# T2 to T4 of the inner values made in place by GpSimd in a pair's second half, and the last pair's splits put in front

## The chip, the core and the metric

The kernel runs on one core of one Trainium2 chip. A core has a matrix engine (TensorE, in the rows PE, its weight loads PEld), a vector engine (VectorE, DVE), a scalar engine (ScalarE, ACT), GpSimd (POOL), and a sync engine (SP) that here only issues DMAs. Each engine takes its own instructions in order; semaphores tie the engines together. Operands lie in SBUF, results of matmuls in PSUM. The metric is the device time of one execution in microseconds; less is better. Three runs of the kernel before gave 1194.9, 1196.52 and 1198.41 us, median 1196.52.

## The reference

Attention in chunks of 64 tokens, then two feed-forward layers over 4608 tokens, all in float32:

```python
scores = scale * q_c @ k_c^T ; attn = softmax(scores) ; x = attn @ v_c      # x: 4608 x 512
h = x @ w_in                                                                # 512 -> 2048
g = h * clip(h + 3, 0, 6) / 6
x = g @ w_out                                                               # 2048 -> 512
h = x @ w_in2 ; solu = h * softmax(h) ; ln = layernorm(solu) * g_ln         # 512 -> 1024
out = ln @ w_out2                                                           # 1024 -> 512
```

## The kernel before

**Precision.** Every float32 operand of a matmul is split into a high part (ScalarE copies it to the faster fp32r type) and a low part (source minus high part, on VectorE or GpSimd). A product is then three matmuls: high by high, high by low, low by high.

**Stages.** The 4608 tokens are 9 blocks of 512. Blocks 0 to 2 go through the first layer plainly (lines 1619 to 1710). Beside their work the kernel forms sums of weight quarters (`sums_of`, `split_sums`) and stores them in HBM (`sti`, `sto`). Blocks 3 to 8 are three pairs, and a pair's first layer is done by Strassen's scheme in Winograd's form: seven products in place of eight. The first two pairs go through `pair_7`, the third through `pair`; then comes the second layer.

**`pair_7`, first half** (line 1356, j from 0 to 7). Seven products per j (`mul7`, line 1164) give four hidden tiles of 128 x 512, which pass through the gate and become the inner values B11, B12, B21 and B22. The second matrix w_out also takes a seven-product form, so the inner values need Winograd's sums as well: T1 = B12 - B11, T2 = B22 - T1, T3 = T2 - B11, T4 = B21 - T2. `later_sums` (line 1335) makes the four on GpSimd as soon as a j is through; T1 stays in SBUF, T2 to T4 go to HBM (`later_t`) by SP's queue.

**`pair_7`, second half** (line 1423). Seven products i, each over eight j. Two j are one wide piece of 128 x 1024, so there are 28 pieces, numbered d = 0 to 27, four to a product. `prepare(d)` splits a piece: ScalarE copies the high part (line 1285), VectorE subtracts for the low part (line 1286); for the pieces 20, 23 and 26 in two halves (1282, 1283). It is issued three pieces ahead of use. `mul_o` (line 1301) then spends 12 matmuls on a piece; the third matmul is the first that reads the low part. `bring` (line 1291) loads T2, T3 and T4 back from HBM into the slots `wo` that the pieces used before have left (`HOMES`). Ten closures in `todo` (made by `prep`, line 1193) are popped at the places in `steps`: they split and subtract the next pair's inputs, on ScalarE (line 1181) and VectorE (1182, 1201). Attention for later blocks is strewn in (`stage`, `att_slot`): transposes on VectorE (490, 494), exponentials on ScalarE (448), scaling on GpSimd (465).

**`pair`, the third pair.** Its w_out products are plain (`moe_o`, line 574), with weights that `load_o` brings from `sto` into the slots `wo`. In the idle places of VectorE and ScalarE it prepares the second layer's weights: `Second.window(words, small)` works on chunks that come by DMA into `xr` (lines 155, 258, 261, 295, 302, 319). What is left of `todo` when it begins is two closures, the splits of B22 and T4.

**Order.** All order is written out by hand (`tc.manual_schedule()`); each engine runs its instructions as the code emits them. TensorE's order is not changed by the diff.

Of the kernel before, what the change touches and what calls it, by code (L numbers as in the profile page):

```python
# [16 lines left out]
P = 128  # L17
# [4 lines left out]
def tile_kernel(  # L22
# [34 lines left out]
    held = nc.dram_tensor("held", (NF, P, BT), F32, kind="Internal").ap()  # L57
    later_t = nc.dram_tensor("later_t", (3, NF // 4, P, 2, BT), F32, kind="Internal").ap()

# [1196 lines left out]
    GROUPS = ("B11", "T1", "B22", "B21")  # L1256
    HOMES = ("B11", "B22", "B21", "B11", "T1", "B22", "B21")
    ND = NJ // 2

    def home(name, m):  # L1260
        return wo_slot(GROUPS.index(name) * ND + m, F32)
# [28 lines left out]

    def bring(d):
        i, m = divmod(d, ND)
        if 0 <= i < 3:
            t = g_t[HOMES[i], m] = home(HOMES[i], m)
            nc.sync.dma_start(out=t, in_=later_t[i, m])

# [14 lines left out]
    def pair_7(p, todo):  # L1311
        b1, b2 = FIRST + 2 * p, FIRST + 2 * p + 1
        base = (b1 + 2) * UPB
        late, made, waiting, coming = None, None, [], []

# [4 lines left out]
        def finish(j, b, c, s1, u2, between):  # L1320
            mul7(b, j, "A22", "T4", False, True)
            nc.vector.tensor_add(out=b, in0=s1, in1=b)
            t = gp_tile("t")
            ramp(b, t)
            between()
            mul7(c, j, "S4", "B22", False, True)
            nc.vector.tensor_add(out=c, in0=u2, in1=c)
            gate(t, b, g_t["B21", j // 2][:, j % 2])
            t = gp_tile("g_hi")
            ramp(c, t)  # L1330
            while waiting:
                waiting.pop(0)()
            return j, t, c

        def later_sums(j, g12):
            m, k = j // 2, j % 2
            g11, g22, g21, t1 = (g_t[n, m][:, k] for n in ("B11", "B22", "B21", "T1"))
            t2, t3, t4 = (work_tile("xo") for _ in range(3))
            sub = nc.gpsimd.tensor_sub
# [16 lines left out]
        for j in range(NJ):  # L1356
# [27 lines left out]
            if j > 1:  # L1384
                made = finish(*late, lambda: stage("norm", u + 1))
            if j == NJ - 1:
                prepare(0)
            if made:
                i, t, ps = made
                gate(t, ps, t)  # L1390
                later_sums(i, t)
            if j != 1:
# [3 lines left out]
            c22 = g_t["B22", m][:, k]  # L1396
            nc.vector.tensor_add(out=c22, in0=u3, in1=c)
            mul7(a, j, "A12", "B21", False, True)
            t = gp_tile("t")
# [11 lines left out]
        prepare(2)  # L1411
        later_sums(i, t)

# [9 lines left out]
        for i in range(len(OUTS)):  # L1423
# [7 lines left out]
            for j in range(NJ):  # L1431
                mul_o(ps, i, j, i in (0, 1, 3, 6), i in (2, 4, 5, 6))
                d = (i * NJ + j) // 2
                if (i, j) == (0, 5):
                    while waiting:
                        waiting.pop(0)()
# [16 lines left out]
                if final:  # L1453
                    if (i, j) == (5, 7):
                        second.append(Second())
                    elif (i, j) in ((6, 4), (6, 7)):
                        second[0].window(1, 0, False)
                    if j % 2 and d % 2 == 0 and d > 2 * ND:
                        load_o(d // 2 - ND - 1)
            for s in range(2):  # L1460
# [36 lines left out]
    def pair(p, todo):  # L1497
        b1, b2 = FIRST + 2 * p, FIRST + 2 * p + 1
        hang, fill = None, second[0]
        for j in range(NJ):  # L1500
            lastj = j == NJ - 1
            if j == 1:
                width.update({"s": 3, "xo": 3})
                fill.places.append(3)
            if 2 * ND + 1 + j < NF:
                load_o(2 * ND + 1 + j)
            a = att_psum()[:, 0]
# [166 lines left out]
    for F in range(2 * NF):  # L1674
# [6 lines left out]
        if F - 2 in UNITS:  # L1681
            split_sums(*UNITS[F - 2], 1)
        for step, u, which in STEPS.get(F, []):
            if step == "turn":
                attn_turn(u, which)
# [15 lines left out]
        if F - 2 in UNITS:  # L1701
            split_sums(*UNITS[F - 2], 0)
        if F in UNITS:
            sums_of(*UNITS[F])
# [141 lines left out]
```

## Time and profile before

| what | value |
|---|---|
| median of 3 runs | 1196.52 us (1194.9 to 1198.41) |
| profiled execution, its own time | 1193.68 us |
| its span in the profile | 1192.0 us |
| TensorE busy | 1169.7 us (98%) |
| VectorE, ScalarE, GpSimd busy | 890.2 (75%), 727.9 (61%), 491.5 (41%) us |
| first half, first pair | about 312 to 399 us |
| second halves of the two pairs | 399.4 to 480.5 and 567.8 to 646.3 us |
| third pair | about 646 to 839 us |
| DMA moved | 258.60 MB; `later_t` has 48 stores of 256 KB and 24 loads of 512 KB |

A row of a timeline has its start (us from the span's start), how long it lasted, engine, line, operation, output and inputs, how many instructions were merged, and in brackets the idle time in front of it and what ended that. An instruction that was started and then held up inside shows as a longer one. PSUM tiles are named `acc`, `att` and `hp`; nearly all others lie in SBUF.

### The profile page before, as it was taken

The numbers are of one execution on the slowest core, as the hardware profiler recorded it, in microseconds if no ns is written. First come the engines' busy times: TensorE is split into PE (matmuls) and PEld (weight loads), VectorE is DVE, ScalarE is ACT, GpSimd is POOL, SyncE is SP. The second block draws the span as 40 slices with busy tenths as digits, with TensorE's granted clock in tenths as the row PEclk, the third lists the DMA queues.
The fourth block names the chain that finished last, engine by engine and source line by source line (L and its number), as shares of the span: only waits on it lengthen the run. The fifth ranks groups of instructions, "written<-read, shape, count | busy, mean of one in ns | idle before, by whom it ended". The sixth has DMA issues, their size and how long they took to land.

```text
span 1192.0 us, 21417 instructions
## 1 busy us (share of the span) xinstructions
PE 1169.7 (98%) x7199; PEld 952.9 (80%) x7199; DVE 890.2 (75%) x1415; ACT 727.9 (61%) x1669; POOL 491.5 (41%) x565
## 2 busy tenths in 40 slices
PE   8999999999999999999999899999999999999998
PEld 6888778788888778787887788888888888888887
DVE  7987667677576987577866666678887878877874
ACT  7775545555465773366644333356886867777775
POOL 1000565443066610275500112101677676765764
PEclk9999999999999999999999899999999999999999
DMA  9901767777689997799999999862322222222311
GB/s 369 381 28 62 241 212 264 239 253 252 243 281 307 313 400 239 242 311 300 336 399 345 351 361 326 306 234 81 128 73 92 79 86 85 79 92 71 99 58 61
DMA packets 172253, 258.60 MB, mean 217 GB/s; under 512 B 19056, under 2 KB 86896, under 8 KB 172144
## 3 DMA queue, kind: packets, MB, share of 16 engines
q1 hardware_dynamic: 159760, 234.69, 57.2%
q10 hardware_dynamic: 12384, 22.55, 5.4%
q8 instruction: 57, 0.93, 0.3%
q14 instruction: 52, 0.43, 0.1%
HBM read 170.40 MB, written 76.02 MB: 207 GB/s over the span
## 4 chain that ended last, share of the span: by engine, by line
PE 91%; DVE 3%; DMA 2%; POOL 1%; ACT 1%; issue 1%; SPq 1%; ACTq 0%; POOLq 0%; DVEq 0%
PE acc L574 17%; PE po L949 16%; PE hp L535 9%; PE acc L1301 9%; PE hp L1164 9%; PE acc L1164 8%; PE b L751 6%; PE c L751 4%; PE a L751 4%; PE hp L1301 3%; PE att L398 3%; PE att L1164 2%; PE att L751 1%; POOL xo L1090 1%; DMA xr<-in_moe_w_in 1%
## 5 line engine op out<-in xcount | busy, mean ns | idle before, releaser
L574 PE MATMUL acc<-g_hi,wo 128*128 128x512 f32 x640 | 163.9, 395 | 0.0
L574 PEld LDWEIGHTS acc<-g_hi,wo 128*128 128x128 f32 x640 | 119.6, 189 | 26.6
L1164 PE MATMUL hp<-wi,w 128*128 128x512 f32 x468 | 119.1, 398 | 7.1 <-ACT wi L319 6.3
L1164 PEld LDWEIGHTS hp<-wi,w 128*128 128x128 f32 x468 | 89.2, 191 | 28.2 <-issue 6.7
L1164 PE MATMUL acc<-wi,w 128*128 128x512 f32 x420 | 104.4, 395 | 2.2 <-DVE tx L1395 2.2
L864 ACT COPY wo<-wo 32x256 f32<-32x256 f32 x228 | 92.1, 404 | 19.2 <-DVE wo L846 11.3
L535 PE MATMUL hp<-x_hi,wi 128*128 128x512 f32 x384 | 97.8, 396 | 0.1
L732 POOL TENSOR_TENSOR x_lo<-xr,x_hi 128x768 fp32r<-128x768 f32 (+1 forms) x30 | 64.1, 2157 | 76.4 <-ACT x_hi L725 76.4
L1301 PE MATMUL acc<-wi,w 128*128 128x512 f32 x408 | 95.3, 392 | 0.0
L1164 PEld LDWEIGHTS acc<-wi,w 128*128 128x128 f32 x420 | 77.9, 188 | 19.5 <-DVE tx L1395 2.5
L1301 PEld LDWEIGHTS acc<-wi,w 128*128 128x128 f32 x408 | 76.5, 188 | 16.8
L448 ACT ACTIVATE p<-att,mx 128x64 f32<-128x64 f32 x256 | 76.6, 320 | 18.8 <-DVE mx L431 16.0
L574 PE MATMUL acc<-g_lo,wo 128*128 128x512 f32 x320 | 87.7, 390 | 0.0
L535 PEld LDWEIGHTS hp<-x_hi,wi 128*128 128x128 f32 x384 | 71.5, 187 | 17.1 <-ACT x_hi L512 0.3
L1286 DVE TENSOR_TENSOR wi<-wo,wi 128x1024 fp32r<-128x1024 f32 x50 | 66.2, 1344 | 24.1 <-ACT wi L1285 23.6
L1285 ACT CAST wi<-wo 128x1024 fp32r<-128x1024 f32 x50 | 51.4, 1065 | 33.4 <-PE hp L1301 16.6
L836 DVE SCALAR_TENSOR_TENSOR wo<-wo,r,wo 128x1024 f32<-128x1024 f32 x36 | 70.3, 1952 | 1.3
L574 PEld LDWEIGHTS acc<-g_lo,wo 128*128 128x128 f32 x320 | 60.1, 188 | 12.8
L933 POOL TENSOR_TENSOR wo<-wo,wo 128x1024 fp32r<-128x1024 f32 x25 | 64.5, 2582 | 6.4 <-ACT wo L929 3.8
L560 POOL TENSOR_TENSOR g_lo<-t,g_hi 128x512 fp32r<-128x512 f32 x15 | 21.4, 1428 | 106.3 <-ACT g_hi L557 98.4
L828 ACT ACTIVATE wo<-wo,nmx 128x1024 f32<-128x1024 f32 x36 | 41.5, 1152 | 22.4 <-DVE nmx L825 22.3
L541 ACT ACTIVATE t<-hp,three 128x512 f32<-128x512 f32 x48 | 33.3, 694 | 35.0 <-PE hp L535 32.4
(319 smaller groups left out, 2848.5 us busy)
## 6 DMA issues: line engine op xcount, KB each, us to landing
w<-sti SPq DMA_DIRECT2D x168, 256.0 KB, 4.8
w<-sto SPq DMA_DIRECT2D x112, 256.0 KB, 5.2
later_t<-xo SPq DMA_DIRECT2D x48, 256.0 KB, 4.6
wo<-later_t SPq DMA_DIRECT2D x24, 512.0 KB, 6.9
wo<-wo SPq DMA_DIRECT2D x328, 32.0 KB, 1.8
x2d<-xo SPq DMA_DIRECT2D x36, 256.0 KB, 4.5
xr<-x2d SPq DMA_DIRECT2D x36, 256.0 KB, 3.3
out<-ob SPq DMA_DIRECT2D x36, 256.0 KB, 2.2
```

What stands on the lines that cost most here:

```text
L448: nc.scalar.activation(out=p_t[u][:, h], in_=sc[:, c, a], func=AF.Exp, scale=0.125, bias=mx[:, m : m + 1], accum_out=sums[u][:, h : h + 1],)
L535: nc.tensor.matmul(hp, wi[f][:, a, kk * P : (kk + 1) * P], b[:, kk], start=(n == 0), stop=(n == 3 * KD - 1),)
L574: nc.tensor.matmul(acc[dc], wo[f][:, w, dc * P : (dc + 1) * P], g[i], start=(at == 0 and n == 0), stop=(at == NF - 1 and n == 2),)
L732: eng.tensor_sub(out=lo[:, f], in0=r, in1=hi[:, f].bitcast(F32))
L751: nc.tensor.matmul(ps, x[:, AT[a], j], w2[w, j][i], start=(start and n == 0), stop=(stop and n == 5), skip_group_check=True,)
L836: nc.vector.scalar_tensor_tensor(out=h, in0=e, scalar=r, in1=h, op0=ALU.mult, op1=ALU.mult, accum_out=mu)
L864: move(out=m[b * 32 : b * 32 + 32, a], in_=tr[a * 32 : a * 32 + 32, b])
L933: eng.tensor_sub(out=lo, in0=m, in1=hi.bitcast(F32))
L949: nc.tensor.matmul(po, a[f], out_w[f][w], start=(n == 0), stop=(n == 3 * NF2 - 1),)
L1164: nc.tensor.matmul(ps, w[:, i, kk * P : (kk + 1) * P], x[:, kk], start=(start and n == 0), stop=(stop and n == 5), skip_group_check=True,)
L1286: nc.vector.tensor_sub(out=e[1], in0=src, in1=e[0].bitcast(F32))
L1301: nc.tensor.matmul(ps[s], w[:, k, s * P : (s + 1) * P], x[l], start=(start and j == 0 and n == 0), stop=(stop and j == NJ - 1 and n == 2), ...
```

## The change

`later_t` goes. In the first half GpSimd makes T1 alone (`first_sum`). T2, T3 and T4 are made in the second half by `in_place`, one GpSimd subtraction of 128 x 1024 for each of four m, written over the slot of B22, B11 and B21; `SUMS_AT` gives the piece d at which each is emitted. In the last step of the first half, `prepare(0)` moves behind two VectorE additions. In `pair`, the first step pops both closures of `todo` before any window, and its windows move behind the sums of the products. Nine of the third pair's sixteen weight slots were loaded in the second half before, four are now; the rest are loaded two to a step. The sums of `sums_of` for odd F move from the end of step F to the front of step F + 1.

```diff
-    HOMES = ("B11", "B22", "B21", "B11", "T1", "B22", "B21")
+    HOMES = ("B11", "B22", "B21", "B22", "T1", "B11", "B21")
...
+    def in_place(n, m):
+        b11, b22, b21, t1 = (g_t[g, m] for g in ("B11", "B22", "B21", "T1"))
+        o, x, y = ((b22, b22, t1), (b11, b22, b11), (b21, b21, b22))[n]
+        nc.gpsimd.tensor_sub(out=o, in0=x, in1=y)
+
+    SUMS_AT = {2 + 2 * m: (0, m) for m in range(ND)}
+    SUMS_AT |= {12 + m: (1, m) for m in range(ND)} | {17 + m: (2, m) for m in range(ND)}
...
-            sub(out=t1, in0=g12, in1=g11)
-            sub(out=t2, in0=g22, in1=t1)
-            sub(out=t3, in0=t2, in1=g11)
-            sub(out=t4, in0=g21, in1=t2)
-            for i, t in enumerate((t2, t3, t4)):
-                waiting.append(
-                    lambda i=i, t=t: nc.sync.dma_start(out=later_t[i, m][:, k], in_=t)
-                )
+        def first_sum(j, g12):
+            g11, t1 = (g_t[n, j // 2][:, j % 2] for n in ("B11", "T1"))
+            nc.gpsimd.tensor_sub(out=t1, in0=g12, in1=g11)
...
-                if j % 2:
-                    bring(d)
-                else:
+                if j % 2 == 0:
                     prepare(d + 3)
+                elif d in SUMS_AT:
+                    in_place(*SUMS_AT[d])
...
-            for _ in todo[:-1]:
+            while todo:
                 todo.pop(0)()
...
-            if not j:
-                fill.window(1, 0)
-            while todo:
-                todo.pop(0)()
-            fill.window(1, 2)
+            if j:
+                fill.window(1, 2)
...
+            if not j:
+                fill.window(1, 0)
             mul7(a, j, "A12", "B21", False, True)
...
-            fill.window(0, 2 * (j > 0), False)
+            fill.window(not j, 2, False)
```

The next two pieces show GpSimd's order from the last step of the first half on, through the first pair's second half; `p` is the scaling of attention, `s` the sums of line 1477. Before:

```order
L1340 TENSOR_TENSOR wo_4580<-g_hi,wo_4579 128x512
L1341 TENSOR_TENSOR xo<-wo_4581,wo_4580 128x512
L1342 TENSOR_TENSOR xo<-xo,wo_4579 128x512
L1343 TENSOR_TENSOR xo<-wo_4582,xo 128x512
L465 TENSOR_TENSOR p<-p,sm 128x512 x3
L1477 TENSOR_TENSOR s<-s 128x512 x2
```

After, GpSimd's order at the same place, from the last `first_sum` to the first T4:

```order
L1336 TENSOR_TENSOR wo_4538<-g_hi,wo_4537 128x512
L464 TENSOR_TENSOR p<-p,sm 128x512
L1293 TENSOR_TENSOR wo_3790<-wo_3790,wo_3789 128x1024
L1293 TENSOR_TENSOR wo_4020<-wo_4020,wo_4019 128x1024
L464 TENSOR_TENSOR p<-p,sm 128x512
L1293 TENSOR_TENSOR wo_4310<-wo_4310,wo_4309 128x1024
L1293 TENSOR_TENSOR wo_4539<-wo_4539,wo_4538 128x1024
L464 TENSOR_TENSOR p<-p,sm 128x512
L1293 TENSOR_TENSOR wo_3788<-wo_3790,wo_3788 128x1024
L1293 TENSOR_TENSOR wo_4018<-wo_4020,wo_4018 128x1024
L1293 TENSOR_TENSOR wo_4308<-wo_4310,wo_4308 128x1024
L1293 TENSOR_TENSOR wo_4537<-wo_4539,wo_4537 128x1024
```

Three narrow subtractions per j have left the first half, and twelve wide ones (four for T2, four for T3, and four for T4 that follow here) stand in the second; in the second pair one scaling stands in front of the twelve and none between them.

VectorE in the last step of the first half of the first pair, before; `hp` and `acc` are PSUM, `wi_4776` is the low part of piece 0:

```order
L1251 SCALAR_TENSOR_TENSOR wo_4582<-t,acc_4568 128x512
L1286 TENSOR_TENSOR wi_4776<-wo_3788,wi_4775 128x1024
L1251 SCALAR_TENSOR_TENSOR g_hi<-g_hi,hp 128x512
L1395 TENSOR_TENSOR tx_4795<-s,acc_4726 128x512
L1397 TENSOR_TENSOR wo_4581<-tx_4795,hp 128x512
```

The same place on VectorE after:

```order
L1250 SCALAR_TENSOR_TENSOR wo_4540<-t,acc_4526 128x512
L1250 SCALAR_TENSOR_TENSOR g_hi<-g_hi,hp 128x512
L1382 TENSOR_TENSOR tx_4731<-s,acc_4675 128x512
L1384 TENSOR_TENSOR wo_4539<-tx_4731,hp 128x512
L1285 TENSOR_TENSOR wi_4735<-wo_3788,wi_4734 128x1024
```

The low part of piece 0 has moved behind the gate and the two additions.

VectorE in the first step of the third pair, before; `xr`, `q`, `v`, `kbd` and `pbd` belong to the second layer's weights, line 1182 is the split of T4:

```order
L1522 TENSOR_TENSOR s<-s,hp 128x512
L258 TENSOR_SCALAR q<-xr_7546 128x512
L261 SCALAR_TENSOR_TENSOR q<-xr_7546,q 128x512
L1182 TENSOR_TENSOR wi_7625<-wi_5873,wi_7624 128x1024
L258 TENSOR_SCALAR v<-xr_7582 128x512
L261 SCALAR_TENSOR_TENSOR v<-xr_7582,v 128x512
L295 TENSOR_TENSOR pbd<-kbd,pbd 128x512
L302 TENSOR_TENSOR v<-v,kbd 128x512
L1533 TENSOR_TENSOR tx_7654<-s,hp 128x512
L1535 TENSOR_TENSOR xo<-tx_7654,hp 128x512
L550 SCALAR_TENSOR_TENSOR t<-t,att 128x512
L1551 TENSOR_TENSOR tx_7684<-s,hp 128x512
```

The same place on VectorE after:

```order
L1181 TENSOR_TENSOR wi_7425<-wi_5783,wi_7424 128x1024
L1509 TENSOR_TENSOR s<-s,hp 128x512
L1517 TENSOR_TENSOR tx_7456<-s,hp 128x512
L1519 TENSOR_TENSOR xo<-tx_7456,hp 128x512
L257 TENSOR_SCALAR q<-xr_7363 128x512
L260 SCALAR_TENSOR_TENSOR q<-xr_7363,q 128x512
L549 SCALAR_TENSOR_TENSOR t<-t,att 128x512
L257 TENSOR_SCALAR v<-xr_7399 128x512
L260 SCALAR_TENSOR_TENSOR v<-xr_7399,v 128x512
L294 TENSOR_TENSOR pbd<-kbd,pbd 128x512
L301 TENSOR_TENSOR v<-v,kbd 128x512
L1537 TENSOR_TENSOR tx_7500<-s,hp 128x512
```

T4's split and the two additions (1533 and 1535, now 1517 and 1519) have moved in front of the work on `xr`; the addition of line 1551 (now 1537) still stands behind it.

## Rows read from the trace of the kernel before

**Rows 1.** The page: busy time (share of the span) and instructions.
```profile
PE 1169.7 (98%) x7199; PEld 952.9 (80%) x7199; DVE 890.2 (75%) x1415; ACT 727.9 (61%) x1669; POOL 491.5 (41%) x565
```

**Rows 2.** Waits of TensorE: total us, times, longest.
```profile
PE hp L1164 <- ACT wi L319: 6.3, 1, 6.3
...
PE acc L1164 <- DVE tx L1395: 2.2, 2, 1.1
...
PE att L398 <- DMA kbd<-in_k: 1.5, 1, 1.5
```

**Rows 3.** Timeline, first step of the third pair.
```profile
651.85 1.54 PE L1164 MATMUL att<-wi,w 128*128 128x512 f32 x6
...
656.30 0.43 DVE L258 TENSOR_SCALAR v<-xr 128x512 int32<-128x512 int32 x1 [0.23 <-DMA xr<-in_moe_w_in]
...
658.88 0.68 DVE L1533 TENSOR_TENSOR tx<-s,hp 128x512 f32<-128x512 f32 x1
...
659.66 5.20 PE L1164 MATMUL hp<-wi,w 128*128 128x512 f32 x12 [6.27 <-ACT wi L319]
...
666.09 2.92 PE L1164 MATMUL hp<-wi,w 128*128 128x512 f32 x12
```

**Rows 4.** Busy time by stretch, ending in granted clock, DMA share and GB/s.
```profile
659.60:664.70 5.10, 5.04 (x12) 3.99 (x13) 2.06 (x3) 2.09 (x4) 1.28 (x1) 0.53 1.01 393
```

**Rows 5.** Timeline, end of the first half of the first pair.
```profile
394.09 1.22 DVE L1286 TENSOR_TENSOR wi<-wo,wi 128x1024 fp32r<-128x1024 f32 x1 [1.16 <-ACT wi L1285]
...
395.83 0.68 DVE L1395 TENSOR_TENSOR tx<-s,acc 128x512 f32<-128x512 f32 x1
...
396.56 1.66 PE L1164 MATMUL acc<-wi,w 128*128 128x512 f32 x6 [1.12 <-DVE tx L1395]
```

**Rows 6.** Timeline of the second half, first pair: SP's queue, then TensorE.
```profile
417.01 0.32 SPq L1295 DMA_DIRECT2D wo<-later_t  x1
...
424.38 0.69 PE L398 MATMUL att<-kbd,q 64*64 64x64 f32 x32 [1.50 <-DMA kbd<-in_k]
```

**Rows 7.** Timeline, VectorE and GpSimd at once, and VectorE alone (last row).
```profile
403.30 3.47 DVE L1286 TENSOR_TENSOR wi<-wo,wi 128x1024 fp32r<-128x1024 f32 x2 [0.25 <-ACT wi L1285]
...
403.37 2.31 POOL L1340 TENSOR_TENSOR wo<-g_hi,wo 128x512 f32<-128x512 f32 x1
...
408.01 1.30 POOL L1342 TENSOR_TENSOR xo<-xo,wo 128x512 f32<-128x512 f32 x1
...
437.62 2.35 DVE L1286 TENSOR_TENSOR wi<-wo,wi 128x1024 fp32r<-128x1024 f32 x2
```

**Rows 8.** Line 933 by engine (ns min/median/max), then the timeline, second layer.
```profile
L933 POOL TENSOR_TENSOR wo<-wo,wo x25: 2390/2415/3416, 840.0 to 1166.4; 128x1024 fp32r<-128x1024 f32 x25
...
925.63 3.42 POOL L933 TENSOR_TENSOR wo<-wo,wo 128x1024 fp32r<-128x1024 f32 x1 [0.22 <-issue]
...
927.02 2.57 DVE L840 TENSOR_SCALAR wo<-wo,mu 128x1024 f32<-128x1024 f32 x1
```

**Rows 9.** Timeline of the first pair's second half: VectorE, then TensorE.
```profile
435.63 2.07 DVE L1182 TENSOR_TENSOR wi<-wi,wi 128x1024 fp32r<-128x1024 f32 x1
...
443.29 1.28 DVE L1201 TENSOR_TENSOR tx<-wi,xr 128x512 f32<-128x512 f32 x2
444.50 1.21 DVE L1286 TENSOR_TENSOR wi<-wo,wi 128x1024 fp32r<-128x1024 f32 x1
...
447.56 11.15 PE L1301 MATMUL hp<-wi,w 128*128 128x512 f32 x48
```

**Rows 10.** Timeline of the second pair's second half: VectorE, then TensorE.
```profile
585.09 1.80 DVE L494 STREAM_TRANSPOSE pbd<-p 32x256 f32<-32x256 f32 x4
...
594.03 1.23 DVE L1286 TENSOR_TENSOR wi<-wo,wi 128x1024 fp32r<-128x1024 f32 x1 [3.61 <-ACT wi L1285]
...
599.72 1.22 DVE L1286 TENSOR_TENSOR wi<-wo,wi 128x1024 fp32r<-128x1024 f32 x1
...
591.29 22.26 PE L1301 MATMUL acc<-wi,w 128*128 128x512 f32 x96
```

More of the change, by code (lines that the diff above doesn't have):

```diff
@@ L57, in tile_kernel @@
     held = nc.dram_tensor("held", (NF, P, BT), F32, kind="Internal").ap()
-    later_t = nc.dram_tensor("later_t", (3, NF // 4, P, 2, BT), F32, kind="Internal").ap()
     const = ctx.enter_context(tc.tile_pool(name="const", bufs=1))
@@ L1289, in prepare @@
             parts_o[i, 2 * m + k] = [t[k] for t in e]
[L1291 to L1295, printed above, removed]
+    def in_place(n, m):
[4 more added lines that the diff above has]
+    SUMS_AT |= {12 + m: (1, m) for m in range(ND)} | {17 + m: (2, m) for m in range(ND)}
     def mul_o(ps, i, j, start, stop):
@@ L1313, in pair_7 @@
         base = (b1 + 2) * UPB
-        late, made, waiting, coming = None, None, [], []
+        late, made, coming = None, None, []
         def load_coming():
@@ L1330, in finish @@
             ramp(c, t)
-            while waiting:
-                waiting.pop(0)()
             return j, t, c
[L1335 to L1339, printed above, removed]
-            sub(out=t1, in0=g12, in1=g11)
-            sub(out=t2, in0=g22, in1=t1)
-            sub(out=t3, in0=t2, in1=g11)
-            sub(out=t4, in0=g21, in1=t2)
-            for i, t in enumerate((t2, t3, t4)):
-                waiting.append(
-                    lambda i=i, t=t: nc.sync.dma_start(out=later_t[i, m][:, k], in_=t)
-                )
+        def first_sum(j, g12):
+            g11, t1 = (g_t[n, j // 2][:, j % 2] for n in ("B11", "T1"))
+            nc.gpsimd.tensor_sub(out=t1, in0=g12, in1=g11)
         def gate_22(j):
@@ L1385, in pair_7 @@
                 made = finish(*late, lambda: stage("norm", u + 1))
-            if j == NJ - 1:
-                prepare(0)
             if made:
@@ L1390, in pair_7 @@
                 gate(t, ps, t)
-                later_sums(i, t)
+                first_sum(i, t)
             if j != 1:
@@ L1397, in pair_7 @@
             nc.vector.tensor_add(out=c22, in0=u3, in1=c)
+            if j == NJ - 1:
+                prepare(0)
             mul7(a, j, "A12", "B21", False, True)
@@ L1411, in pair_7 @@
         prepare(2)
-        later_sums(i, t)
+        first_sum(i, t)
         s1 = [work_tile("s") for _ in range(2)]
@@ L1433, in pair_7 @@
                 d = (i * NJ + j) // 2
-                if (i, j) == (0, 5):
-                    while waiting:
-                        waiting.pop(0)()
-                if j % 2:
-                    bring(d)
-                else:
+                if j % 2 == 0:
                     prepare(d + 3)
+                elif d in SUMS_AT:
+                    in_place(*SUMS_AT[d])
                 if (i, j) in steps:
@@ L1457, in pair_7 @@
                         second[0].window(1, 0, False)
-                    if j % 2 and d % 2 == 0 and d > 2 * ND:
-                        load_o(d // 2 - ND - 1)
+                    if j % 2 and d % 2 == 0 and d >= 5 * ND:
+                        load_o(d // 2 - 2 * ND - 2)
             for s in range(2):
@@ L1504, in pair @@
                 fill.places.append(3)
-            if 2 * ND + 1 + j < NF:
-                load_o(2 * ND + 1 + j)
+            for f in range(2 * j + ND, 2 * j + ND + 2):
+                if f < NF:
+                    load_o(f)
             a = att_psum()[:, 0]
@@ L1682, in tile_kernel @@
             split_sums(*UNITS[F - 2], 1)
+        if F - 1 in UNITS and F % 2 == 0:
+            sums_of(*UNITS[F - 1])
         for step, u, which in STEPS.get(F, []):
@@ L1702, in tile_kernel @@
             split_sums(*UNITS[F - 2], 0)
-        if F in UNITS:
+        if F in UNITS and F % 2 == 0:
             sums_of(*UNITS[F])
```

## The prediction, made before the changed kernel ran

> **What bounds the kernel now.** I read the page's busy line first: TensorE is busy 1169.7 of 1192.0 us [rows 1], and its order stays as it was. So a gain can only be a wait of TensorE that goes, and a loss only a wait that comes. The list of TensorE's waits is therefore next. Three of them touch the change [rows 2]: 6.3 us once, 1.1 us twice, and 1.5 us once. The timelines at these places say what ends each.
>
> The 6.3 us are in the first step of the third pair. The product A12 by B21 ends at 653.39 (651.85 + 1.54), the next starts at 659.66 [rows 3]. The list names ScalarE's line 319, but the product adds onto a PSUM tile that VectorE's addition of line 1533 still has to read, and that addition ends at 659.56, 0.1 us before TensorE goes on. It stands behind a chunk of second-layer weights whose DMA lands only at 656.30 [rows 3]. After the wait twelve matmuls take 5.20 us at a granted clock of 0.53 [rows 3, 4], about the lower of the two levels, 1.2 GHz; elsewhere 48 take 11.15, so twelve take 2.75 [rows 9].
>
> The 1.1 us come once in each of the first two pairs: the addition of line 1395 stands behind the low part of piece 0 [rows 5]. The 1.5 us are a load of k that SP issued late, since the load of a later sum in front of it went out only at 417.01 [rows 6].
>
> **What goes.** Line 1395 now stands in front of the low part: 1.1 us in each pair, 2.2. Piece 0 is not needed until the block after that, so nothing is late in its place. The loads and stores of `later_t` leave SP's queue, k is issued in time: 1.5. No TensorE wait in the list ends with GpSimd's sums of the first half, so taking three subtractions per step from there gives nothing by itself.
>
> In the third pair line 1533 follows its product at once, and T4 has been split by then, so the 6.3 us and the slow clock (5.20 - 2.75 = 2.45) go. What is late next is the addition of line 1551, which still stands behind the chunk of 656.30: in front of it on VectorE are then four operations of up to 0.64 us (half of the 1.28 in rows 9) and ScalarE's shift of the raw words between the first two, and GpSimd's low part of a gate beside them: 656.3 + 5 x 0.64 + 1.3, I put its end at about 660.8. The first product of the next step that needs its tile then starts there, and not at 666.09 [rows 3]: 5.3 us gained. The bounds are 8.7 (all of 6.27 + 2.45) and 3.
>
> Gains: 2.2 + 1.5 + 5.3 = 9.0 us, between 6 and 12.5.
>
> **What comes.** In each of the two pairs, twelve wide subtractions on GpSimd stand in the second half, where VectorE makes the low parts that TensorE's third matmul of each piece waits for. What happens when both engines work on SBUF is in the timeline [rows 7]. Two low parts, alone, take 2.35 us. With GpSimd's narrow subtraction beside them two took 3.47, 1.12 more, and that subtraction 2.31, while an undisturbed one takes 1.30. The times fit a strict turn: VectorE's first until 404.4, GpSimd's until 405.7 (403.37 + 2.31), VectorE's second until 406.8 (403.30 + 3.47). Neither runs beside the other, and each lets the other in after one instruction. It holds for a wide one too: GpSimd's of 925.63 ends at 929.05, and VectorE's of 927.02 ends only at 929.59 [rows 8].
>
> The Trainium skill says this as a rule (SBUF — State Buffer, "Who interferes with whom"): a VectorE instruction with two SBUF inputs contends with a GpSimd instruction that reads SBUF, and the one that comes second is blocked for the whole of the first. The trace agrees: the 1.12 us above are nearly a whole subtraction of 1.30. By the rule the twelve operations stand in VectorE's time and the sum is the one below; if the two engines only shared bandwidth, the sum would come to the faster rival.
>
> The price of one: no f32 output of this width is in the trace. The nearest is line 933, same width, least 2.39 and median 2.42 us [rows 8]; twice the undisturbed narrow one is 2.6. I take 2.4. Ends: 2.3 and 2.6.
>
> First pair. GpSimd's third scaling holds T3 and T4 back until about the subtraction of line 1182 at 435.63. From there VectorE has eight operations with two SBUF inputs before the low part of piece 18 at 444.50: that split, four low parts, a wide subtraction and two narrow ones (443.29) [rows 7, 9]. In each gap one wide GpSimd operation goes in: 8 x 2.4 = 19.2 us. Piece 18 is the third of its product, whose block starts at 447.56 [rows 9]; its low part is wanted at 447.56 + 2 x 2.75 + 0.46 (two matmuls) = 453.5 and was there at 445.7, 7.8 us early. TensorE and VectorE both move ahead by the 2.6 us gained before, which leaves that lead. So TensorE loses 19.2 - 7.8 = 11.4 us. It loses them in several waits; the last, in front of piece 18, has three GpSimd operations in it (one after piece 17's low part and one after each narrow subtraction): 3 x 2.4 + 2 x 0.6 + 1.1 - 2.75 = 6.8 us. That is as long as the wait after which the clock stood at 0.53, so I add 2.4. Then GpSimd is through, and VectorE catches up.
>
> Second pair. Only one scaling stands in front, so all twelve follow each other from piece 4 on, and eleven are in front of the low part of piece 14: 26.4 us. Piece 14 is the seventh of the eight in TensorE's block that starts at 591.29: wanted at 591.29 + 6 x 2.75 + 0.46 = 608.2, there at 600.9, 7.3 early [rows 10]. VectorE had 3.6 us idle before 594.03, which are filled, and I let one GpSimd operation, 2.4 us, run beside the transposes around 585 [rows 10], which read one tile only. The narrow sums that cost VectorE 3.47 - 2.35 = 1.1 us at the start are gone. So 26.4 - 7.3 - 3.6 - 2.4 - 1.1 = 12.0 us. I add no clock here: the waits are 4.4 us and less, and what a slower clock takes there is partly taken from the next wait. Bounds for the clock in both pairs together: 0 and 7.
>
> Losses: 11.4 + 2.4 + 12.0 = 25.8 us. The ends: nothing, if the leads take all of it up, and 34, with 2.6 us for each of the nineteen operations counted (3.8 more) and the clock at its upper end (4.6 more).
>
> At nothing I cost: the 72 transfers of `later_t` (TensorE waits for no weight tile of the ring now); the five weight slots that move into the third pair, since each is asked for three steps of the pair before its use; the sums of odd F, which stand half a step later than before and beside which TensorE has no wait in the list. If the moved loads stood in a full queue, the chunks of the second layer would come later, and the 5.3 us would shrink.
>
> **The sum.** 1193.68 (the profiled execution; span 1192.0 and 1.7 around it) - 9.0 + 25.8 = 1210.5 us. The profiled execution is 2.8 below the median of the timed runs, and below all three; so the median may lie up to 3 us above the sum. I say 1211.
>
> **Rivals.**
> Faster: GpSimd's operations don't stand in VectorE's way, because VectorE's lead of 7 us and its idle times take them up. Then only the gains count: 1193.7 - 9.0 = 1184.7, on the median's scale 1187. For it: VectorE is busy 75% overall [rows 1], and the pieces have a lead. Against: the lead is 7 us, eight or eleven operations of 2.4 stand in it, and from 435.6 to 445.7 VectorE goes from one operation to the next [rows 9]. It turns into a loss once more than about three operations per pair (7.3 / 2.4) stand in front of a low part.
> No change: the turns are not strict, VectorE passes with two low parts to one GpSimd operation. Then half of the operations stand in front of the late low part: 4 x 2.4 - 7.8 = 1.8 in the first pair and 13.2 - 7.3 = 5.9 in the second, against 9.0 gained: 1192.4, or 1195 on the median's scale. Against it: rows 7 show the turn after every instruction.
> Worse: the clock falls in each of the long waits (7 us in all, not 2.4), and the third pair gains 3 instead of 5.3: 1210.5 + 4.6 + 2.3 = 1217.4, or 1220 on the median's scale. For it: rows 4 show what one such wait costs; against: the other waits are 4.4 us and less, and no row shows the clock falling after one of that length.
> The change does not do what it says: line 1533 is free but T4's split is late, so the wait stays. T4's copy now stands behind one copy out of PSUM only, so I see no ground for it; it is in the case before.
>
> **How the numbers follow.** The forecast (1203 to 1217) 0.64, the faster rival 0.15, no change 0.11, worse 0.10. What a measurement of this kernel can tell from no change is about 0.3%, 3.6 us: within are 1192.9 to 1200.1. So faster 0.15, same 0.11, slower 0.74, the last from the forecast and the worse case. Range 1191 to 1220: it takes in no change and most of the worse case, and leaves out the faster rival.
>
> **What the profile after will show.** Right: TensorE waits for line 1285's low parts (by VectorE) around pieces 14 to 18 of the first pair and 10 to 15 of the second, with low parts that last 3 us and more in the row and GpSimd's line 1293 that last 3.5; the waits of lines 1395 and of k gone; the wait of the third pair's first step down to some 3 us. Wrong: line 1293 at 2.4 each and low parts at 1.2, or TensorE busy without a gap through both second halves.

## The result, and the profile after

The changed kernel takes 1213.58 us, median of four runs (1212.62 to 1216.51), against 1195.8 (1194.9 to 1198.41) for the kernel before: ratio 1.0149, 95% interval 1.0125 to 1.0173. It is slower, by 1.5%. The forecast was 1211, in a range from 1191 to 1220. The profiled execution took 1212.62 us, its span is 1210.8 (before 1192.0).

Line numbers are one to sixteen lower now: 1286 is 1285, 1301 is 1302 (one higher), 1395 is 1382, 1533 is 1517, 1551 is 1537. Line 1293 is the new subtraction of GpSimd. From the page of after come the busy line and two of the costliest groups (busy us, mean ns of one, idle before):

```profile
PE 1179.8 (97%) x7199; PEld 956.6 (79%) x7199; DVE 932.3 (77%) x1415; ACT 728.0 (60%) x1669; POOL 500.2 (41%) x541
...
L1285 DVE TENSOR_TENSOR wi<-wo,wi 128x1024 fp32r<-128x1024 f32 x50 | 97.3, 1965 | 7.9 <-ACT wi L1284 7.5
...
L1293 POOL TENSOR_TENSOR wo<-wo,wo 128x1024 f32<-128x1024 f32 x24 | 77.1, 3246 | 0.0
```

The line of the low parts on the page of before:

```profile
L1286 DVE TENSOR_TENSOR wi<-wo,wi 128x1024 fp32r<-128x1024 f32 x50 | 66.2, 1344 | 24.1 <-ACT wi L1285 23.6
```

The same fifty low parts that took 66.2 us now take 97.3: they are the same work, held up inside. TensorE has as many instructions as before, and is busy 10 us longer ([rows 1]); 9.4 of them go with a lower clock in the second halves, as shown below.

TensorE's waits after (total us, times, longest):

```profile
PE hp L1302 <- DVE wi L1285: 7.5, 2, 3.9
PE acc L1302 <- DVE wi L1285: 6.2, 6, 3.6
PE att L397 <- ACT p L447: 4.5, 3, 2.1
PE hp L1163 <- DVE tx L1537: 2.7, 1, 2.7
...
PE hp L1163 <- DVE s L1509: 0.8, 1, 0.8
```

The three waits of [rows 2] are gone or smaller: none for line 1382, none for k, and 2.7 us in the third pair in place of 6.3. Line 1285's are new. To see what each is worth, I cut both spans at the starts of TensorE's blocks (first product of a half, first plain product of the next; before, the first of these is at 310.5 us and not at about 312):

| stretch | before | after | difference | predicted |
|---|---|---|---|---|
| start to the first product of pair 1 | 310.50 | 312.30 | +1.80 | 0 |
| first half, pair 1 | 88.93 | 87.76 | -1.17 | -1.1 |
| second half, pair 1 | 81.09 | 92.79 | +11.70 | +12.3 (13.8 - 1.5) |
| first half, pair 2 | 87.24 | 86.05 | -1.19 | -1.1 |
| second half, pair 2 | 78.59 | 88.63 | +10.04 | +12.0 |
| third pair and all behind it | 545.65 | 543.27 | -2.38 | -5.3 |
| span | 1192.0 | 1210.8 | +18.8 | +16.8 |

**The turn.** The timeline of after in the first pair's second half, VectorE, GpSimd and TensorE, answers to [rows 9]:

```profile
437.50 25.53 POOL L1293 TENSOR_TENSOR wo<-wo,wo 128x1024 f32<-128x1024 f32 x8
438.54 6.76 DVE L1285 TENSOR_TENSOR wi<-wo,wi 128x1024 fp32r<-128x1024 f32 x2
...
445.23 3.43 DVE L1200 TENSOR_TENSOR xr<-xr,xr 128x1024 f32<-128x1024 f32 x1
...
448.58 6.66 DVE L1285 TENSOR_TENSOR wi<-wo,wi 128x1024 fp32r<-128x1024 f32 x2
451.99 8.24 PE L1302 MATMUL hp<-wi,w 128*128 128x512 f32 x24 [3.60 <-DVE wi L1285]
455.16 5.67 DVE L1200 TENSOR_TENSOR tx<-wi,xr 128x512 f32<-128x512 f32 x2
460.75 3.36 DVE L1285 TENSOR_TENSOR wi<-wo,wi 128x1024 fp32r<-128x1024 f32 x1
...
464.17 6.87 PE L1302 MATMUL hp<-wi,w 128*128 128x512 f32 x22 [3.94 <-DVE wi L1285]
...
465.24 1.21 DVE L1285 TENSOR_TENSOR wi<-wo,wi 128x1024 fp32r<-128x1024 f32 x1
```

Eight GpSimd subtractions run in one row without a gap, and VectorE does exactly eight operations with two inputs from SBUF beside them, the last of them the low part of piece 18: one, then one. Two low parts take 6.76 us where two alone take 2.35 [rows 7], so a turn costs (6.76 - 2.35) / 2 = 2.2 us. At 463.0 GpSimd is through, and the next low part takes 1.21 again. The second pair shows the same with twelve:

```profile
591.93 39.09 POOL L1293 TENSOR_TENSOR wo<-wo,wo 128x1024 f32<-128x1024 f32 x12
...
598.91 13.27 DVE L1285 TENSOR_TENSOR wi<-wo,wi 128x1024 fp32r<-128x1024 f32 x4
...
618.87 8.40 PE L1302 MATMUL acc<-wi,w 128*128 128x512 f32 x24 [3.61 <-DVE wi L1285]
...
632.17 2.11 PE L1302 MATMUL acc<-wi,w 128*128 128x512 f32 x8 [0.30 <-DVE wi L1285]
```

**Waits and clock.** The stretches of the two second halves, before and then after (start and end, us, busy us of TensorE with its instructions, of the weight loads, VectorE, ScalarE and GpSimd, then granted clock, DMA share and GB/s):

```profile
399.40:480.50 81.10, 79.60 (x465) 65.02 (x464) 65.00 (x80) 45.76 (x99) 20.20 (x12) 1.00 0.90 318
567.80:646.30 78.50, 78.50 (x401) 64.01 (x400) 60.46 (x72) 41.72 (x67) 16.41 (x10) 1.00 1.00 360
```

```profile
400.06:492.85 92.79, 84.78 (x466) 67.58 (x464) 83.99 (x80) 45.98 (x100) 48.58 (x19) 0.94 0.63 192
578.90:667.53 88.63, 82.73 (x402) 65.50 (x401) 83.01 (x73) 41.97 (x68) 46.05 (x17) 0.96 0.65 200
...
452.00:460.20 8.20, 8.20 (x24) 6.21 (x24) 8.20 (x3) 0.62 (x1) 8.20 (x3) 0.68 0.30 82
```

In the first pair TensorE waits 92.79 - 84.78 = 8.0 us and is busy 5.2 longer; in the second it waits 5.9 and is busy 4.2 longer. After the wait of 3.60 us, 24 matmuls take 8.24 us at a granted clock of 0.68, where 24 take 5.6 elsewhere. So 9.4 of the 23 us lost look like work. They come from waits all the same, and most of them are not on top: a matmul that runs slowly in front of a late low part shortens the next wait by as much.

**The third pair's first step.** Timeline of after, VectorE, ScalarE and TensorE, answering to [rows 3]:

```profile
670.71 1.23 DVE L1181 TENSOR_TENSOR wi<-wi,wi 128x1024 fp32r<-128x1024 f32 x1 [2.29 <-ACT wi L1180]
...
671.85 0.68 DVE L1509 TENSOR_TENSOR s<-s,hp 128x512 f32<-128x512 f32 x1
672.59 1.65 PE L1163 MATMUL hp<-wi,w 128*128 128x512 f32 x6 [0.77 <-DVE s L1509]
...
674.27 0.69 DVE L1517 TENSOR_TENSOR tx<-s,hp 128x512 f32<-128x512 f32 x1 [1.74 <-PE hp L1163]
...
676.85 0.62 ACT L318 CAST wi<-q 128x512 fp32r<-128x512 f32 x1 [2.52 <-DVE q L260]
677.37 0.68 ACT L1229 ACTIVATE t<-att,three 128x512 f32<-128x512 f32 x1
...
678.09 0.69 DVE L549 SCALAR_TENSOR_TENSOR t<-t,att 128x512 f32<-128x512 f32 x1 [1.27 <-ACT t L1229]
678.69 0.42 DVE L257 TENSOR_SCALAR v<-xr 128x512 int32<-128x512 int32 x1
...
680.03 1.31 DVE L260 SCALAR_TENSOR_TENSOR v<-xr,v 128x512 int32<-128x512 int32 x1 [0.92 <-ACT xr L154]
...
682.46 0.67 DVE L1537 TENSOR_TENSOR tx<-s,hp 128x512 f32<-128x512 f32 x1
...
683.19 4.32 PE L1163 MATMUL hp<-wi,w 128*128 128x512 f32 x12 [2.70 <-DVE tx L1537]
```

A stretch from here, with the granted clock as its third number from the end:

```profile
683.03:686.03 3.00, 2.84 (x7) 2.26 (x8) 2.69 (x5) 1.81 (x3) 0.69 (x1) 0.50 1.09 390
```

Line 1517 no longer stands behind the words. Line 1537 does, TensorE waits 2.70 us for it, and the twelve matmuls behind take 4.32 us in place of 2.75, with the clock at 0.50 in the first three. T4's split in front now costs 0.77 us.

### The profile page after: what moved, and what is told of

The parts are those of the page before. It is cut to its first block, busy times and chain, and to the rows that moved or that the text cites. A ratio compares the mean times of both kernels' runs of the same rounds, so it can differ in the third digit from the quotient of the medians.

```text
span 1210.8 us, 21226 instructions
## 1 busy us (share of the span) xinstructions
PE 1179.8 (97%) x7199; PEld 956.6 (79%) x7199; DVE 932.3 (77%) x1415; ACT 728.0 (60%) x1669; POOL 500.2 (41%) x541
## 4 chain that ended last, share of the span: by engine, by line
PE 83%; DVE 8%; DMA 3%; issue 3%; POOL 2%; ACT 1%; SPq 0%; ACTq 0%; POOLq 0%; DVEq 0%
PE po L948 16%; PE acc L573 15%; PE hp L534 9%; PE acc L1163 8%; PE hp L1163 7%; PE acc L1302 6%; PE b L750 5%; PE c L750 4%; PE a L750 4%; DVE wi L1285 3%; PE att L397 2%; PE hp L1302 2%; PE att L1163 1%; PE att L750 1%; DMA w<-sti 1%
## 5 line engine op out<-in xcount | busy, mean ns | idle before, releaser
L1302 PE MATMUL acc<-wi,w 128*128 128x512 f32 x408 | 100.1, 402 | 6.4 <-DVE wi L1285 6.2
L1163 PE MATMUL acc<-wi,w 128*128 128x512 f32 x420 | 104.4, 395 | 0.0
L1285 DVE TENSOR_TENSOR wi<-wo,wi 128x1024 fp32r<-128x1024 f32 x50 | 97.3, 1965 | 7.9 <-ACT wi L1284 7.5
L1293 POOL TENSOR_TENSOR wo<-wo,wo 128x1024 f32<-128x1024 f32 x24 | 77.1, 3246 | 0.0
L1342 POOL TENSOR_TENSOR wo<-g_lo,wo 128x512 f32<-128x512 f32 x16 | 20.8, 1298 | 108.4 <-ACT g_lo L1247 104.4
```

What stands on the lines that cost most here:

```text
L1163: nc.tensor.matmul(ps, w[:, i, kk * P : (kk + 1) * P], x[:, kk], start=(start and n == 0), stop=(stop and n == 5), skip_group_check=True,)
L1285: nc.vector.tensor_sub(out=e[1], in0=src, in1=e[0].bitcast(F32))
L1293: nc.gpsimd.tensor_sub(out=o, in0=x, in1=y)
L1302: nc.tensor.matmul(ps[s], w[:, k, s * P : (s + 1) * P], x[l], start=(start and j == 0 and n == 0), stop=(stop and j == NJ - 1 and n == 2), ...
```

## The experiments

My theory was the prediction's: GpSimd and VectorE take strict turns over reads of SBUF, and what stands in a row in front of a late low part, less VectorE's lead, is the loss. The rivals were a shared rate, a cost for each GpSimd operation wherever it stands, and something else in the change. The ratios are to the kernel before on the same chip in the same session (its medians were 1193.64 to 1194.72 us). The last columns, in us, are from one profiled execution each.

| run | median us | ratio, 95% interval | start to pair 1 | second halves | third pair on |
|---|---|---|---|---|---|
| e1_no_sums | 1191.45 | 0.9982 (0.9973 to 0.9992) | 313.93 | 79.63, 78.69 | 545.46 |
| e2_narrow | 1207.41 | 1.0115 (1.0095 to 1.0135) | 312.70 | 89.10, 83.60 | 548.32 |
| e3_vector | 1193.54 | 0.9992 (0.9980 to 1.0005) | 312.32 | 80.05, 78.90 | 546.33 |
| e4_front | 1189.53 | 0.9963 (0.9948 to 0.9978) | 309.67 | 81.88, 78.57 | 543.29 |
| e5_memset | 1191.34 | 0.9973 (0.9962 to 0.9984) | 311.86 | 79.63, 78.70 | 544.21 |
| e6_sums_back | 1213.68 | 1.0162 (1.0146 to 1.0178) | 311.04 | 93.56, 90.25 | 543.81 |
| e7_front_later | 1190.85 | 0.9963 (0.9950 to 0.9975) | 310.22 | 81.03, 78.68 | 543.92 |
| e8_vector_later | 1189.44 | 0.9962 (0.9949 to 0.9976) | 309.97 | 80.05, 78.90 | 544.98 |
| e9_t2_gpsimd | 1192.37 | 0.9984 (0.9974 to 0.9993) | 309.94 | 80.74, 78.88 | 548.87 |
| e10_vector_back | 1191.18 | 0.9974 (0.9965 to 0.9984) | 309.77 | 80.05, 78.89 | 548.00 |

**Without the subtractions.** In `in_place`:

```diff
-        nc.gpsimd.tensor_sub(out=o, in0=x, in1=y)
+        return
```

> The kernel after with the 24 GpSimd subtractions of line 1293 left out, so T2 to T4 are not formed and their pieces hold other values; all else as after. Theory (the subtractions hold VectorE's low parts up): the 13.2 and 10.0 us that the two second halves lost go, and the result is 1213.6 - 23.2 = 1190.4 us, 1188 to 1192; TensorE waits for line 1285 no more in the two second halves. Rival (the loss comes from something else in the change: the order of the splits, the weight slots loaded later, the loads of k): the time stays above 1205.

The two second halves lose 13.16 and 9.94 us of their length: the two losses, 13.2 and 10.0. No wait for line 1285 is left. The median lies in the range, but on the scale of before's 1195.8 the ratio means 1193.6 us, 3 more than reckoned. The profiled execution, itself 1.9 above this run's median, has 1.6 us more before pair 1 and 2.2 more behind the pairs than that of after; 1.2 of the 2.2 are a slower clock behind the same wait, as the last section shows. The stretches, not the sum, carry what follows.

**A write in place of a subtraction.**

```diff
-        nc.gpsimd.tensor_sub(out=o, in0=x, in1=y)
+        nc.gpsimd.memset(o, 0.5)
```

> The kernel after with each of GpSimd's 24 subtractions of line 1293 replaced by a GpSimd memset of the same tile to 0.5, at the same place: it writes the same 128x1024 and reads nothing; T2 to T4 are not formed. Theory (the turn is over reading: GpSimd's reads of SBUF keep VectorE's two-input operations out): VectorE's low parts stay at 1.2 us and the time is that of the kernel with the subtractions left out, 1190 to 1193 us. Rival (any GpSimd instruction on these tiles, a write too, takes the turn, or the waits between the two engines cost the time): low parts of 2 us and more beside the memsets, TensorE waits for line 1285, and over 1200 us.

The lines of this run:

```profile
L1285 DVE TENSOR_TENSOR wi<-wo,wi 128x1024 fp32r<-128x1024 f32 x50 | 64.5, 1307 | 23.9 <-ACT wi L1284 23.5
...
L1293 POOL MEMSET wo<- 128x1024 f32 x24 | 21.8, 952 | 4.7 <-DVE wi L1285 4.6
```

The low parts have the 1307 ns that they have without any subtraction (64.5 us, 1307 ns in e1_no_sums too), though GpSimd writes the same tiles at the same places. So what blocks is that GpSimd reads, not that it runs or that its tiles are waited for. The Trainium skill says the same (SBUF — State Buffer, "Who interferes with whom"): a VectorE operation with two SBUF inputs contends with a GpSimd operation that reads SBUF, not with one that only writes it. The memset is also shorter (952 ns), but 21.8 us of it left no trace in the low parts at all.

**The same work in narrower pieces.**

```diff
-        nc.gpsimd.tensor_sub(out=o, in0=x, in1=y)
+        for k in range(2):
+            nc.gpsimd.tensor_sub(out=o[:, k], in0=x[:, k], in1=y[:, k])
```

> The kernel after with each subtraction of line 1293 cut into two of 128x512: the same GpSimd work in 48 instructions of some 1.3 us in place of 24 of 2.4 or more. Theory (strict turn: one GpSimd instruction goes in after each VectorE instruction with two SBUF inputs): what stands in front of piece 18's low part falls from 8 x 3.2 to 8 x 1.5 or so, against a lead of 7.8: the first pair loses about 4 in place of 13.2, the second 2 or less in place of 10, and the result is about 1196 us, 1193 to 1201. Rival (the two engines share a rate, and only GpSimd's sum of time counts): as after, 1212 to 1215.

Neither number came: 1207.4. The timeline of this run (GpSimd, VectorE, TensorE):

```profile
436.85 32.69 POOL L1294 TENSOR_TENSOR wo<-wo,wo 128x512 f32<-128x512 f32 x16
...
437.89 4.56 DVE L1285 TENSOR_TENSOR wi<-wo,wi 128x1024 fp32r<-128x1024 f32 x2
...
454.85 5.33 PE L1303 MATMUL hp<-wi,w 128*128 128x512 f32 x22 [1.62 <-DVE wi L1285]
...
466.21 3.04 PE L1303 MATMUL acc<-wi,w 128*128 128x512 f32 x12 [2.82 <-DVE wi L1285]
```

The turn is confirmed, and a shared rate is not: two low parts take 4.56 us, so a turn now costs 1.1, half as much; if the two engines shared a rate, a low part would be slowed alike beside wide and narrow pieces. At piece 18 TensorE waits 1.62 us, no more than I had reckoned. But the row of turns lasts twice as long in operations (sixteen in place of eight, to 469.5), and the next product's low parts stand in it: 2.82 us, and more behind. My expectation had stopped counting at piece 18. Smaller pieces spread the same loss over more low parts and save a part of it.

**The same subtractions on VectorE.**

```diff
-        nc.gpsimd.tensor_sub(out=o, in0=x, in1=y)
+        nc.vector.tensor_sub(out=o, in0=x, in1=y)
```

> The kernel after with the 24 wide subtractions of line 1293 done by VectorE, at the same places of the code. Theory (what costs is that GpSimd and VectorE keep each other out; a wide subtraction of VectorE's takes 1.22 us [rows 5]): in front of piece 18 stand 8 x 1.22 = 9.8 us against a lead of 7.8, in front of piece 14 of the second pair 11 x 1.22 = 13.4 against 7.3 + 3.6 + 1.1: 2.0 + 1.4 us lost, 1190.4 + 3.4 = 1194 us, 1190 to 1197. Rival (VectorE's own time is what runs out, whoever subtracts; or the pieces wait for the sums themselves): over 1203, with waits of TensorE for line 1285 as long as after.

1193.5, as expected. Against no subtractions at all the second halves lose 0.42 and 0.21 us, less than the 2.0 and 1.4 that I had: VectorE has the room there for 24 more operations of 1.3 us. It did not have it for GpSimd's reads. The whole cost is larger: the medians of e3_vector and e1_no_sums, from one session, lie 2.1 us apart, and in the third pair TensorE waits 3.3 us for line 1509 in e3_vector, 1.0 in e1_no_sums.

**T2 on GpSimd, T3 and T4 on VectorE; the sums of odd F back in their old place** in this and the next run:

```diff
-        nc.gpsimd.tensor_sub(out=o, in0=x, in1=y)
+        (nc.vector if n else nc.gpsimd).tensor_sub(out=o, in0=x, in1=y)
```

> The kernel after with T2 made in place by GpSimd (four wide subtractions for each pair, spread over the first twelve pieces), T3 and T4 in place by VectorE, and the sums of odd F at their old place. Theory (what costs is a row of GpSimd subtractions behind which a late low part stands, since each turn takes 2.2 us of VectorE's lead; where they stand two at a time with scalings between them the lead of 7 us takes them up): TensorE waits for no low part of line 1285, and the time is that of the kernel with all sums on VectorE, sent with this, or up to 1 us less. Rival (each GpSimd subtraction costs TensorE its own price of some 2 us wherever it stands): eight in all, 10 to 16 us more than the kernel sent with this.

> The kernel after with T2 to T4 made in place by VectorE and the sums of odd F at their old place; the third pair's first step as in the kernel after. Theory (the later place of the sums costs some 2 us in the first 312 us, which the second halves don't take back here, since no late low part stands there): a ratio to the kernel before of 0.9992 - 0.0018 = 0.9974, first product of pair 1 near 310.2 us. Rival (the early gain falls away later, as it did with GpSimd's subtractions): 0.9990.

In e9_t2_gpsimd the second pair's four stand in one row:

```profile
577.48 12.47 POOL L1293 TENSOR_TENSOR wo<-wo,wo 128x1024 f32<-128x1024 f32 x4
```

They take 3.1 us each, so they are in turns too, and the second half is 78.88 us long, against 78.89 with VectorE alone. In the first pair it is 0.69 longer, with waits for line 1285 of 0.4 us. Eight times 2 us, the rival's price, did not come. An operation in turns is free as long as a lead is there to take it up. I had expected no wait at all, or a gain; a small loss came.

e10_vector_back gave 0.9974, what the later place of the sums was expected to cost; its interval just overlaps that of e3_vector, so the ratios alone do not settle it. Both kernels pay in the third pair for what VectorE took over. Timeline of e10_vector_back there, ScalarE, VectorE and TensorE:

```profile
645.88 0.59 ACT L1497 COPY s<-att 128x512 f32<-128x512 f32 x1 [2.50 <-DVE xo L1466]
...
647.44 1.23 DVE L1181 TENSOR_TENSOR wi<-wi,wi 128x1024 fp32r<-128x1024 f32 x1 [1.07 <-ACT wi L1180]
648.59 0.68 DVE L1509 TENSOR_TENSOR s<-s,hp 128x512 f32<-128x512 f32 x1
...
649.32 2.07 PE L1163 MATMUL hp<-wi,w 128*128 128x512 f32 x6 [2.54 <-DVE s L1509]
```

ScalarE waits for VectorE's last outputs of the second half, T4's split comes late, line 1509 stands behind it, and TensorE waits 2.54 us, where in after it was 0.77.

**The sums of odd F back, nothing else.**

```diff
-        if F - 1 in UNITS and F % 2 == 0:
-            sums_of(*UNITS[F - 1])
...
-        if F in UNITS and F % 2 == 0:
+        if F in UNITS:
             sums_of(*UNITS[F])
```

> The kernel after with the sums of the weight quarters for odd F put back to the end of step F. Theory: in the plain blocks GpSimd's scaling stood behind nothing before, and the later place of the sums is what makes three attention products wait in the first 200 us; put back, pair 1 starts at 310 us in place of 312.3 (before 310.5), and the result is 1.8 us less, 1211.8, 1210.5 to 1213. Rival: those waits are the spread of executions, and nothing changes: 1213.6.

The time did not fall. Pair 1 did start earlier, at 311.04, and what was won went in the second halves (+0.8 and +1.6 in its profiled execution). The late low parts come at the same place as in after: TensorE goes on with piece 18 at 64.15 us into the first pair's half (after: 64.11) and with piece 14 at 49.90 into the second's (49.93). What is longer lies behind them. In the first pair it is the clock: 0.56 in the 5.6 us behind that wait, where after has 0.69. In the second pair it is so for about 1.0 of the 1.6 (0.78 in 7.7 us, where after has 1.00); the rest is spread over the pieces that follow, without a cause in the trace. In both, the wait itself was the longer one (4.82 us for 3.94, 2.75 for 1.55). One execution does not show whether this is the rule. The early part, however, is the same code in many runs: with the sums late five executions start pair 1 at 311.86 to 313.93 (mean 312.6), with the sums in their old place seven start it at 309.67 to 311.04 (mean 310.2). TensorE's waits there for the exponentials that are over 1 us, in after and then before:

```profile
145.86 0.69 PE L397 MATMUL att<-kbd,q 64*64 64x64 f32 x32 [1.34 <-ACT p L447]
...
172.81 0.69 PE L397 MATMUL att<-kbd,q 64*64 64x64 f32 x32 [2.10 <-ACT p L447]
...
188.25 0.69 PE L397 MATMUL att<-kbd,q 64*64 64x64 f32 x32 [1.03 <-ACT p L447]
```

```profile
172.50 0.83 PE L398 MATMUL att<-kbd,q 64*64 64x64 f32 x32 [2.73 <-ACT p L448]
```

The trace shows a tie at the first of them. `sums_of` begins with two additions on VectorE (line 1074) into tiles that GpSimd's splits of the sums before (line 1089) still read. In after these additions start at 134.94, after 3.95 us of waiting for that split, before at 133.26. The maxima that the exponentials need (line 430) stand behind them on VectorE and follow at 139.41, before at 137.74.

**The two other parts alone**, in the kernel before: `prepare(0)` behind the two additions, and the third pair's first step as in after; T2 to T4 still go through memory.

```diff
-            if j == NJ - 1:
-                prepare(0)
             if made:
...
             nc.vector.tensor_add(out=c22, in0=u3, in1=c)
+            if j == NJ - 1:
+                prepare(0)
...
-            for _ in todo[:-1]:
+            while todo:
                 todo.pop(0)()
...
-            fill.window(0, 2 * (j > 0), False)
+            fill.window(not j, 2, False)
```

> The kernel before, with two parts of the change alone: the split of piece 0 behind the two additions, and in the third pair's first step both closures in front and the windows behind. T2 to T4 go through memory as before. Theory: the two parts are worth what the stages of after showed for them, 2 x 1.15 for the first (1.17 and 1.19) and 2.4 for the second, against 1195.8: 1191.1 us, 1189 to 1193. Rival by the prediction's own working: the second is worth 5.3 where the loads of the second layer's words come early, 1188 us. Rival: T4's way through memory makes its split late in front, the wait of 6.3 stays, 1193.5 us.

0.9963, the 1191.1 us of the theory (1191.1 / 1195.8 = 0.9961). These parts of the change are a gain, and the kernel with them alone beats both.

**The window still later.** In e4_front, and with VectorE's sums and the old place of `sums_of` in e8_vector_later:

```diff
-            while todo:
+            for _ in todo[:-1]:
                 todo.pop(0)()
...
             nc.vector.tensor_add(out=u2, in0=s1, in1=b)
+            while todo:
+                todo.pop(0)()
...
-            fill.window(not j, 2, False)
+            if j:
+                fill.window(0, 2, False)
...
             nc.vector.tensor_add(out=c12, in0=u2, in1=c)
+            if not j:
+                fill.window(1, 2, False)
```

> The kernel of the run with the two parts alone (splits in front, T2 to T4 through memory), and in the third pair's first step one thing more: T4's split stands behind the addition after S2 by T2 (0.8 us waited there), and the second window stands behind the step's last addition (line 1556 there) in place of in front of the addition of line 1550. Theory (a term of 5.3 gave 2.4 because the addition of line 1550 was held by the window's words, 2.7 us of wait and 1.5 to 2.5 us at the lower clock after it): these go, 4 to 6 us less than 1189.5, so 1184 to 1186 us. Rival: the wait moves to the next step, whose windows stand behind the one delayed, and the time stays at 1188 to 1190.

> T2 to T4 made in place as in the kernel after, but by VectorE; the sums of odd F at their old place; the third pair's first step with T4's split and the second window later, as in the run sent with it. Theory: the terms add up: 1193.5 (VectorE's subtractions) - 1.8 (sums back) - 4 to 6 (third pair) = 1187 us, 1185 to 1189. Rival: the second halves have no slack left on VectorE, T4's sums and splits come late in the third pair, and the gain there falls away: 1190 to 1193.

Waits of e7_front_later in the third pair:

```profile
PE hp L1164 <- DVE s L1522: 3.9, 3, 2.2
PE hp L1164 <- DVE tx L1532: 1.2, 1, 1.2
```

The wait of 2.7 us and the slow clock behind it are gone; 5.1 us of waits in the next steps stand in their place, for additions that are now behind the delayed words. The rival was right: the stretch from the third pair on is 543.92, no shorter than 543.29. The words are due work on VectorE, and in this run the later place only chose who waited. e8_vector_later reached 0.9962, by ratio 1191.3 us where 1187 was expected: the sum of the terms failed by this one.

## Why the prediction was right, step by step

**Right.** The addition in front of the low part: 1.1 us a pair predicted, 1.17 and 1.19 measured, and again 1.2 in every run that has it. The load of k: its wait is gone, and without the subtractions the second half is 1.46 shorter. The strict turn: e5_memset and e2_narrow show it, by the reads and by the width. T4's copy came early enough for line 1517, as I had said; but line 1509 and TensorE waited 0.77 us for the split, which I had at nothing. One of the rows that I read the turn from is of another kind than the rule: line 840 [rows 8] has one wide tile as its input, not two.

**Right by two errors that cancel: the first pair.** Piece 18's third matmul starts 64.11 us into the half, before 54.1, or 52.6 without k's wait: 11.5 late, predicted 11.4. A turn cost 2.2 in place of 2.4, which takes 1.6 off. But I let VectorE move ahead with TensorE, and it did not: its two low parts start 38.19 us into the half before and 38.48 after, so the 1.5 of k came out of the lead. The clock after the last wait added 1.8 (22 matmuls in 6.87 us where 5.1 is usual), predicted 2.4; that wait was 3.94 us, where I had 6.8, since another of 3.60 stood in front of piece 16.

**Mis-sized: the second pair.** 10.0 in place of 12.0. Eleven turns at 2.2 are 2.2 us less. I had said that no row shows the clock falling after waits of 4.4 us and less. It fell after 3.6 us here. The trace of before held a case too, which I had not read: behind the wait of 2.73 us that ends at 172.50 the clock stood at 0.56 for 3.5 us. The rule I gave held, though: what the slow clock takes is taken from the next wait, and only what comes after the last one is on top.

**Failed: the end of the addition of line 1551, which I put at about 660.8.** That made 5.3 us; 2.4 came, below my lower bound of 3. The twelve matmuls behind it start 15.66 us into the stretch (683.19 - 667.53), not 14.45, and run at the lower clock, 4.32 us in place of 2.75: 5.3 - 1.2 - 1.6 = 2.5. I had left a wait of some 3 us there, but no slow clock behind it. How much clock such a wait costs differs from one execution to the next, so the 1.6 are not a price to build on.

The 1.2 us come from the operations in front. I let them start with the landing of the second chunk, and from its first operation to the end of line 1537 they took 4.4 us (678.69 to 683.13), as I had reckoned (4.5). But they start 11.16 us into the stretch, not 9.95: the gate of line 549, which stood behind the words before, now stands in front, and it waits for ScalarE, which first converts the first chunk. The chunk's own landing does not set it: in after, e1_no_sums, e4_front, e5_memset and e6_sums_back it lands from 9.98 to 11.20 us into the stretch, and line 1537 (1550 in e4_front) starts at 14.93 to 15.01 in all five. Nor do the moved loads, my reservation: e4_front has them in their old place.

**Failed: the sums of odd F, costed at nothing** because TensorE had no wait beside them. It had one, of 2.73 us, and has three now, of 4.47 together: 1.8 us in the profiled execution, 2.4 by the means of five and seven. That these waits end with ScalarE's exponentials, while the sums are made by VectorE and GpSimd, hid the tie from me.

Together, from the predicted +16.8: +2.9 (third pair), +1.8 (sums), -2.0 (second pair), -0.6 (first pair), -0.1: +18.8. Of the rivals, the faster one had the two leads and VectorE's idle time taking the operations up; e9_t2_gpsimd shows that they do for four in a row, and after that they don't for eight or twelve.

Open: whether the sums' old place gains anything in a kernel whose second halves wait, since e6_sums_back won 1.3 us in front and lost 2.4 behind, in one execution; and what TensorE's clock does after a wait of 2.7 us, which differs between executions of the same code.

## What to carry to other kernels

Moving work to an idle engine is not free when it reads SBUF while VectorE reads two inputs there: here 24 GpSimd subtractions made the two second halves 23 us longer, and the same 24 on the busier VectorE 0.6 (some 2 us in the whole kernel). Reckon such a loss as the length of the row in front of the late operation less its lead, and go on counting behind the first late one. A wait that ends on deferred work moves with that work, so look at who stands behind it in the new place.

## What the runs showed of the hardware that I had not expected

TensorE's granted clock fell after waits of 2.7 us in some executions and not in others. The same twelve matmuls behind the wait of line 1537, in e1_no_sums and in e6_sums_back, answering to the last row of after's third pair above:

```profile
661.78 5.49 PE L1163 MATMUL hp<-wi,w 128*128 128x512 f32 x12 [2.77 <-DVE tx L1537]
```

```profile
684.41 3.03 PE L1163 MATMUL hp<-wi,w 128*128 128x512 f32 x12 [2.71 <-DVE tx L1537]
```

They took 5.49 us at a granted clock of 0.50 in e1_no_sums, 4.32 in after, 4.24 in e4_front, and 3.03 at 1.00 in e6_sums_back, 2.75 being usual; the waits were 2.77, 2.70, 2.73 and 2.71. So the price of the same wait was 0.3 to 2.7 us, from one execution to the next.

Behind a GpSimd operation in a row of turns VectorE's narrow operations pay as much as wide ones: two of 128x512 took 5.67 us beside wide subtractions, 1.28 alone [rows 9].
